# First token group of a fused convolution and MLP kernel: rows of four tokens per partition, taps transposed and added on TensorE

## Chip, cores and metric

One core of a Trainium2 chip runs the whole kernel. The metric is device time in microseconds; 1181.46 us is the median of three runs of the kernel before (1181.32 to 1181.98). A profile is one execution of the same program.

## What is computed

For each of 16384 tokens (4 sequences of 4096) a softmax over 7 taps is formed for each of 8 heads; the token's 192 features are the sum over the taps of weight times the features of the token and the six before it. The result goes through an MLP with 2048 hidden units whose activation is s * relu(h)^2 + b.

```python
w = np.exp(weight_gen - np.max(weight_gen, axis=-1, keepdims=True))
w = w / (np.sum(w, axis=-1, keepdims=True) + 1e-09)          # softmax over K = 7 taps
x_unf = x_pad[:, idx, :].reshape(B, S, K, H, group)          # the token and the six before it
x = np.einsum('bshk,bskhg->bshg', w, x_unf).reshape(B * S, D)  # D = 192, H = 8, group = 24
h = x @ w_in                                                 # w_in 192 x 2048, float64
r = np.maximum(h, 0.0)
out = ((s * (r * r) + b) @ w_out).astype(np.float32)         # w_out 2048 x 192, float64
```

## The kernel before, in words

**Tiling.** Tokens come in 32 groups of 512 (`T`), taken in the order 1 to 31, then 0. A group goes through the convolution on DVE, is transposed, and is multiplied with the weights on PE. The hidden units come in 16 blocks of 128; two blocks are a chunk (`NC` = 8 chunks), with one tile `wc[i]` per chunk that holds a high and a low part of its weights.

**Precision.** Each product is made of three fp32r matmuls: high weights by high x, low weights by high x, high weights by low x. `convert(i)` makes the parts of a chunk from the raw float64 words in four steps: Abs on ACT (L187); three DVE steps (L190 to L198); the high copy on ACT (L203) beside two DVE steps (L205, L209); six matmuls on PE (L219 to L221) that leave the low part in PSUM, and the copy of it on ACT (L222). `ahead(i, n)` issues the next n of these steps.

**Layout of a group.** In `load` a partition holds 16 tokens and 48 of the 192 features (a quarter, `q`), with six tokens of halo. `conv_pieces(g)` is a list of 15 small pieces: softmax_a, exp, softmax_b, four products (L300), five adds (L311, L319), the DVE transposes (L330, L335), split_hi on ACT (L342) and split_lo on DVE (L348). The result stands in two tiles: xa has the first 32 features of each quarter, 128 in all; xb has the other 16 of each, 64 in all, and the same 64 a second time in the other half of the partitions, put there by copies through DMA, which SP issues (L355). xb is multiplied in two halves of 64 partitions.

**Order of work.** Everything stands under `manual_schedule`: each engine, and each engine's list of DMA issues, runs in the order of the program text. SP issues nearly all transfers. First come the loads of group 0 (x by ACT's queue), the raw weights of chunks 0 and 1 (`load_weights(0)`), group 1, the raw weights of chunks 2 and 3, s and b; then group 0's convolution with chunk 0's conversion between its pieces; then a loop over the 8 chunks that does group 0's MLP (`mm1_pair`, `relu2`, `low_g`, `mm2_pair`) beside the conversion of the next chunks and the convolution of group 1. From group 1 on `mm1_quad` and `mm2_quad` take two chunks at a time. In `relu2` ACT does Relu (L443), Square (L445), then a conversion step's low copy, then gh (L449); `low_g` is one DVE instruction (L455).

**Places that the change touches.** The first loads (L535 to L541), `load_weights` (L149), `conv_pieces` (L262), `mm1_pair` (L402), the calls ahead of the chunk loop (L549 to L554), and `store` (L523). The program gives all transfers of SP and ACT eight completion semaphores, handed out in turn; a transfer is issued only when the one that had its semaphore before has landed.

Of the kernel before, what the change touches and what calls it, by code (L numbers as in the profile page):

```python
# [7 lines left out]
F32 = mybir.dt.float32  # L8
F32R = mybir.dt.float32r
# [11 lines left out]
def dynamic_conv_then_relu2_mlp(  # L21
# [24 lines left out]
    nc = tc.nc  # L46
# [27 lines left out]
    xin = ctx.enter_context(tc.tile_pool(name="xin", bufs=2))  # L74
    conv = ctx.enter_context(tc.tile_pool(name="conv", bufs=1))
# [15 lines left out]
    ORDER = list(range(1, NG)) + [0]  # L91

# [56 lines left out]
    def load_weights(k):  # L149

        r = raw.tile([P, 2, CW, 2], U32, tag="r", name="r")
        rw = r.rearrange("p c n w -> p c (n w)")
        c0 = k * QUAD * P * 2
        for q in range(Q):
            src = w_in_u[q * FQ:q * FQ + 1, c0:c0 + 1]
            nc.sync.dma_start(
                out=rw[q * 32:(q + 1) * 32, :, CA * 2:CB * 2],
                in_=bass.AP(src.tensor, src.offset, [[F * 2, 32], [2 * P * 2, 2], [1, 2 * P * 2]]),
            )
        for q in range(Q):  # L160
            for i in range(2):
                f = (q + 2 * i) % Q * FQ + 32
                c = c0 + (1 - q // 2) * P * 2
                src = w_in_u[f:f + 1, c:c + 1]
                nc.sync.dma_start(
                    out=rw[q * 32 + i * TAIL:q * 32 + (i + 1) * TAIL, :, CB * 2:CO * 2],
                    in_=bass.AP(src.tensor, src.offset, [[F * 2, TAIL], [2 * P * 2, 2], [1, P * 2]]),
                )
        for c in range(2):
            o = (k * 2 + c) * 2 * P  # L170
# [5 lines left out]
        raw_t[k] = r  # L176
# [47 lines left out]

    def constants():
# [35 lines left out]

    def conv_pieces(g):  # L262
        st = {}

        def softmax_a():
            wg = wg_t.pop(g)
            w = wg.rearrange("p j h k -> p (j h) k")
# [11 lines left out]
        def softmax_b():  # L279
# [5 lines left out]
            w = small.tile([P, J, HQ, K], F32, tag="w", name="w")  # L285
# [58 lines left out]
        def split_lo():  # L344
# [8 lines left out]
            for q in range(Q):  # L353
                o = (q + 2) % Q * 32
                nc.sync.dma_start(out=b[q * 32 + TAIL:q * 32 + 2 * TAIL], in_=b[o:o + TAIL])  # L355

            x_t[g] = [[(0, v[:, 0]), (1, v[:, 0]), (0, v[:, 1])] for v in x]

        return [
# [281 lines left out]
```

## Time and profile before

| | |
|---|---|
| median of three runs | 1181.46 us (1181.32 to 1181.98) |
| span of the profiled execution | 1178.3 us |
| PE busy | 1144.9 us, 97% |
| DVE busy | 938.2 us, 80% |
| ACT busy | 826.4 us, 70% |
| PE busy from 0 to 10, 10 to 20, 20 to 30, 30 to 40, 40 to 50 us | 0, 1.76, 4.90, 8.00, 9.14 us |

A row of the timeline gives the start in us, the length in us, the engine (PEld is PE's weight load, SPq and ACTq are DMA issues), the line, the operation, output and input by name, and a count where like instructions are merged. A bracket at its end is the idle time before it and what ended it. In a table by stage each engine has its busy time with the number of instructions behind it.

### The profile page before, as it was taken

The page shows a single profiled execution, that of the slowest core. Times are in us where ns is not written, and L with a number is a line of the kernel's source. Part 1 is how long each engine was busy: PE and PEld are TensorE (multiplying, and loading weights), DVE is VectorE, ACT ScalarE, POOL GpSimd, SP SyncE. Part 2 cuts the span into 40 slices and gives each one's busy share as a digit, 9 for nine tenths or more (in the row PEclk, how much of TensorE's full clock was granted, in tenths as well). Part 3 has the DMA queues.
Part 4 walks back from the last instruction along what each step waited for, and adds up shares of the span by engine and source line. Part 5 has one row for each costly group of instructions (what it writes and reads, how often), then busy time and mean ns, then how long its engine had stood idle before and what let it go on. Part 6 is the DMA issues. An engine that isn't in the chain of part 4 may idle for free.

```text
span 1178.3 us, 29855 instructions
## 1 busy us (share of the span) xinstructions
PE 1144.9 (97%) x12672; PEld 1034.5 (88%) x12672; DVE 938.2 (80%) x1357; ACT 826.4 (70%) x889; POOL 6.1 (1%) x22
## 2 busy tenths in 40 slices
PE   2999999999999999999999999999999999999997
PEld 1678999999999999999999999999999999999997
DVE  7988887788887778887778898777788777888843
ACT  2767767777677677776776776767767677677674
POOL 0000000000000000000000000000000000000000
PEclk9999999999999999999999999999999999999999
DMA  7421222221122222122222112222112222212110
GB/s 155 117 44 28 40 46 47 32 46 27 35 46 46 39 40 37 30 40 47 46 33 46 26 36 46 46 35 44 29 37 42 47 46 33 45 26 36 24 24 14
DMA packets 175833, 50.17 MB, mean 43 GB/s; under 512 B 165076, under 2 KB 168660, under 8 KB 175700
## 3 DMA queue, kind: packets, MB, share of 16 engines
q1 hardware_dynamic: 172820, 47.73, 22.6%
q8 instruction: 99, 1.62, 0.6%
q10 hardware_dynamic: 2880, 0.54, 0.3%
q14 instruction: 34, 0.28, 0.1%
HBM read 27.26 MB, written 12.58 MB: 34 GB/s over the span
## 4 chain that ended last, share of the span: by engine, by line
PE 95%; DVE 2%; ACT 1%; DMA 1%; SPq 0%; issue 0%
PE po L500 47%; PE ph L432 43%; PE po L482 2%; PE ph L219 1%; PE ph L408 1%; DVE pr L300 1%; PE ph L414 1%; DMA r<-in_moe_w_in_dram 0%; DVE gl L455 0%; DVE pr L311 0%; ACT gh L449 0%; PE ph L246 0%; ACT r L445 0%; SPq L101 0%; DMA xb<-xb 0%
## 5 line engine op out<-in xcount | busy, mean ns | idle before, releaser
L500 PE MATMUL po<-wc,gh 64*128 64x384 f32 x3936 | 570.5, 356 | 0.0
L500 PE MATMUL po<-wc,gl 64*128 64x192 f32 x3936 | 492.8, 247 | 0.8 <-DVE gl L455 0.8
L455 DVE TENSOR_TENSOR gl<-r,gh 128x1024 fp32r<-128x1024 f32 x256 | 313.1, 1223 | 213.1 <-ACT gh L449 206.9
L443 ACT ACTIVATE r<-ph 128x1024 f32<-128x1024 f32 x256 | 249.0, 1024 | 300.0 <-PE ph L432 295.1
L500 PEld LDWEIGHTS po<-wc,gl 64*128 64x128 f32 x3936 | 375.7, 188 | 6.3 <-DVE gl L455 1.1
L500 PEld LDWEIGHTS po<-wc,gh 64*128 64x128 f32 x3936 | 368.7, 184 | 5.1
L432 PE MATMUL ph<-xa,wc 64*128 64x512 f32 x2976 | 365.6, 391 | 0.0
L432 PEld LDWEIGHTS ph<-xa,wc 64*128 64x128 f32 x2976 | 269.8, 184 | 52.9 <-issue 0.2
L449 ACT CAST gh<-r 128x1024 fp32r<-128x1024 f32 x256 | 269.2, 1052 | 7.9
L445 ACT ACTIVATE r<-r 128x1024 f32<-128x1024 f32 x256 | 270.7, 1057 | 0.3
L300 DVE TENSOR_TENSOR pr<-xt,w 128x1152 f32<-128x1152 f32 (+1 forms) x128 | 193.6, 1554 | 2.5 <-DMA r<-in_moe_w_in_dram 0.7
L432 PE MATMUL ph<-xb,wc 64*128 64x512 f32 x1488 | 190.4, 388 | 0.0
L432 PEld LDWEIGHTS ph<-xb,wc 64*128 64x128 f32 x1488 | 139.9, 184 | 30.5
L311 DVE TENSOR_TENSOR pr<-pr 128x768 f32<-128x768 f32 (+1 forms) x128 | 145.2, 1155 | 2.1
L512 DVE SCALAR_TENSOR_TENSOR u<-po,s_sb,bias 128x192 f32<-128x192 f32 x128 | 49.8, 410 | 1.6 <-PE po L482 1.6
L518 DVE SCALAR_TENSOR_TENSOR y<-po,s_sb,u 128x192 f32<-128x192 f32 x128 | 49.8, 409 | 0.1
L219 PE MATMUL ph<-r,eye_f 128*128 128x384 f32 x32 | 15.6, 570 | 18.2 <-DVE r L198 18.2
L319 DVE TENSOR_TENSOR acc<-pr 128x768 f32<-128x768 f32 x32 | 30.6, 958 | 1.1
L330 DVE STREAM_TRANSPOSE xT<-acc 128x128 f32<-128x128 f32 x128 | 28.5, 280 | 1.1
L335 DVE STREAM_TRANSPOSE xT<-acc 128x128 f32<-128x128 f32 x128 | 27.2, 271 | 0.0
L482 PE MATMUL po<-wc,gh 128*128 128x384 f32 x80 | 23.9, 361 | 0.1
L219 PEld LDWEIGHTS ph<-r,eye_f 128*128 128x128 f32 x32 | 5.7, 205 | 20.8 <-issue 20.8
(45 smaller groups left out, 336.0 us busy)
## 6 DMA issues: line engine op xcount, KB each, us to landing
xt<-in_x_dram SPq DMA_DIRECT2D x120, 132.0 KB, 3.4
out_dram<-y SPq DMA_DIRECT2D x128, 96.0 KB, 1.9
xb<-xb SPq DMA_DIRECT2D x128, 64.0 KB
wg<-in_weight_gen_dram SPq DMA_DIRECT2D x128, 28.0 KB, 2.6
r<-in_moe_w_out_dram SPq DMA_DIRECT2D x8, 384.0 KB, 3.7
r<-in_moe_w_in_dram SPq DMA_DIRECT2D x16, 128.0 KB, 3.0
r<-in_moe_w_in_dram SPq DMA_DIRECT2D x32, 32.0 KB, 2.2
xt<-in_x_dram ACTq DMA_DIRECT2D x4, 132.0 KB, 4.0
```

What stands on the lines that cost most here:

```text
L219: nc.tensor.matmul(out=o, lhsT=eye_f, rhs=fv[:, c], start=True, stop=False)
L300: nc.vector.tensor_tensor(out=pr[:, k0:k1, :, h * G:(h + 1) * G], in0=bass.AP(xs.tensor, xs.offset, [xs.ap[0], [FQ, n], [FQ, J], [1, G]]), ...
L311: nc.vector.tensor_tensor(out=pr[:, o:o + n], in0=pr[:, o:o + n], in1=pr[:, a:a + n], op=ALU.add)
L432: nc.tensor.matmul(out=h_t[n, p][:, j], lhsT=w1(2 * k + p, part, block, j, rows), rhs=v[rows], start=(at < 2 and c == 0), stop=(at >= 4 an ...
L443: nc.scalar.activation(out=r[p], in_=h_t.pop((n, p)), func=AF.Relu)
L445: nc.scalar.activation(out=r[p], in_=r[p], func=AF.Square)
L449: nc.scalar.copy(out=gh, in_=r[p])
L455: nc.vector.tensor_tensor(out=gl, in0=sq, in1=gh.bitcast(F32), op=ALU.subtract)
L482: nc.tensor.matmul(**m)
L500: nc.tensor.matmul(**m)
L512: nc.vector.scalar_tensor_tensor(out=u[i], in0=o_t[g][tiles[i]][:, 1, :], scalar=s_sb, in1=bias, op0=ALU.mult, op1=ALU.add,)
L518: nc.vector.scalar_tensor_tensor(out=y[:, t], in0=o_t[g][t][:, 0, :], scalar=s_sb, in1=u[i - 1], op0=ALU.mult, op1=ALU.add,)
```

## The change

Group 0 of the processing order gets a path of its own. `load_rows` puts four neighbouring tokens with all 192 features (and six tokens of halo) in a partition, by one transfer for the tap weights and two for x, all on SP. The products are made for all taps by `times` (tails: features 32 to 47 of each quarter, per token; firsts: features 0 to 31, per range of taps), and `sum_taps` transposes each tap's product on PE and adds the taps in PSUM. ACT and DVE then split the sums from PSUM into xa and xb (`row_hi`, `row_lo`); the second half of xb is filled by one DMA copy on SP, asked for after the tails and ahead of the firsts. `load_weights` can take one chunk at a time and issue its block B on another queue: chunk 0's goes to ACT's queue. A one-column Exp is done right after the constants, and `awake()` puts 48 matmuls on PE. `mm1_pair` of chunk 0 does the high weights of both blocks first, then the six convert matmuls and the low copy of chunk 0, then the low weights. The store of group 0 is one transfer.

```diff
--- before.py
+++ after.py
@@ -72,6 +72,7 @@
+    rows = ctx.enter_context(tc.tile_pool(name="rows", bufs=1))
@@ -89,6 +90,23 @@
+
+    def load_rows(i):
+
+        t0 = ORDER[i] * T
+        wg = xin.tile([P, NT, H, K], F32, tag="wg", name="wg")
+        nc.sync.dma_start(
+            out=wg.rearrange("p a h k -> p (a h k)"),
+            in_=wgf[t0:t0 + T, :].rearrange("(p a) n -> p (a n)", a=NT),
+        )
+        xt = rows.tile([P, NT + HALO, D], F32, tag="xr", name="xr")
+        src = xf[t0 - HALO:t0 - HALO + 1, :]
+        for a0, a1 in ((0, 2 * NT - 1), (2 * NT - 1, NT + HALO)):
+            nc.sync.dma_start(
+                out=xt[:, a0:a1].rearrange("p a d -> p (a d)"),
+                in_=bass.AP(src.tensor, src.offset + a0 * D, [[NT * D, P], [1, (a1 - a0) * D]]),
+            )
+        xt_t[i], wg_t[i] = xt, wg
@@ -146,34 +164,47 @@
-    def load_weights(k):
...
+    def load_weights(k, chunks=(0, 1), side=nc.sync):
+
+        if k not in raw_t:
+            raw_t[k] = raw.tile([P, 2, CW, 2], U32, tag="r", name="r")
+        a, n = chunks[0], len(chunks)
+        rw = raw_t[k].rearrange("p c n w -> p c (n w)")
+        c0 = (k * 2 + a) * 2 * P * 2
+        rw = rw[:, a:a + n]
+
+        def block_a(q):
+            f = q * FQ
+            src = w_in_u[f:f + 1, c0:c0 + 1]
             nc.sync.dma_start(
...
+                in_=bass.AP(src.tensor, src.offset, [[F * 2, 32], [2 * P * 2, n], [1, 2 * P * 2]]),
+            )
+        def block_b(q, i):
+            f = (q % 2 + 2 * i) * FQ + 32
+            c = c0 + (1 - q // 2) * P * 2
+            src = w_in_u[f:f + 1, c:c + 1]
+            side.dma_start(
+                out=rw[q * 32 + i * TAIL:q * 32 + (i + 1) * TAIL, :, CB * 2:CO * 2],
+                in_=bass.AP(src.tensor, src.offset, [[F * 2, TAIL], [2 * P * 2, n], [1, P * 2]]),
+            )
...
+        for q in range(Q):
+            block_a(q)
+        for q in range(Q):
+            for i in range(2):
+                block_b(q, i)
+        for c in range(n):
+            second_weights(c)
@@ -222,6 +253,14 @@
+    spare = const.tile([P, 1], F32, name="spare")
+
+    def awake():
+
+        ph = ps_h.tile([P, 2, T], F32, tag="h1", name="ph")
+        for _ in range(48):
+            nc.tensor.matmul(out=ph[:, 0, 0:P], lhsT=eye, rhs=ones, start=True, stop=True)
@@ -259,11 +298,78 @@
+    def parts_of(x):
+        return [[(0, v[:, 0]), (1, v[:, 0]), (0, v[:, 1])] for v in x]
...
+        def times(out, f, k0, n, slot, m, each, width):
+
+            xs, ws = xt_t[g][:, k0 + slot:k0 + slot + 1, f:f + 1], st["w"][:, slot:slot + 1, f // G:f // G + 1, k0:k0 + 1]
+            nc.vector.tensor_tensor(
+                out=out,
+                in0=bass.AP(xs.tensor, xs.offset, [xs.ap[0], [D, n], [each * G, m], [1, width]]),
+                in1=bass.AP(ws.tensor, ws.offset, [ws.ap[0], [1, n], [each * K, m], [0, width]]),
+                op=ALU.mult,
+            )
+
+        def sum_taps(i, k0, k1, a):
+            m = (P, P // 2)[i]
+            for k in range(k0, k1):
+                nc.tensor.matmul(
+                    out=st["ps"][i][0:m, a * P:(a + 1) * P], lhsT=st["p"][i][:, k, a], rhs=eye_f,
+                    is_transpose=True, start=(k == 0 and a == 0), stop=(k == K - 1), skip_group_check=True,
+                )
+
+        def row_tails(a):
+            def f():
+                if a == 0:
+                    pr = conv.tile([P, K * NT * D], F32, tag="pr", name="pr")
+                    n = K * NT * P
+                    st["p"] = [v.rearrange("p (k a n) -> p k a n", k=K, a=NT) for v in (pr[:, 0:n], pr[:, n:])]
+                    st["ps"] = [ps_o.tile([P, T], F32, tag=f"o{i}", name="px") for i in range(2)]
+                out = st["p"][1][:, :, a].rearrange("p k (o e n) -> p k o e n", o=2, e=2)
+                for e in range(2):
+                    times(out[:, :, :, e], 32 + e * 2 * FQ, 0, K, a, 2, 2, TAIL)
+                sum_taps(1, 0, K, a)
+            return f
+
+        def row_firsts(k0, k1):
+            def f():
+                out = st["p"][0][:, k0:k1].rearrange("p k a (q n) -> p k (a q) n", q=Q)
+                times(out[:, :, :, 0:G], 0, k0, k1 - k0, 0, NT * Q, 2, G)
+                times(out[:, :, :, G:32], G, k0, k1 - k0, 0, NT * Q, 2, 32 - G)
+                for a in range(NT):
+                    sum_taps(0, k0, k1, a)
+            return f
+
+        R = [slice(0, P), slice(0, P // 2)]
+
+        def row_hi(i):
+            def f():
+                if "x" not in st:
+                    st["x"] = [xtp.tile([P, 2, T], F32R, tag=n, name=n) for n in ("xa", "xb")]
+                nc.scalar.copy(out=st["x"][i][R[i], 0], in_=st["ps"][i][R[i]])
+            return f
+
+        def row_lo(i):
+            def f():
+                x = st["x"][i]
+                nc.vector.tensor_tensor(
+                    out=x[R[i], 1], in0=st["ps"][i][R[i]], in1=x[R[i], 0].bitcast(F32), op=ALU.subtract
+                )
+                if i == 1:
+                    b = x.bitcast(F32)
+                    nc.sync.dma_start(out=b[P // 2:P], in_=b[0:P // 2])
+                else:
+                    xt_t.pop(g)
+                    x_t[g] = parts_of(st["x"])
+            return f
@@ -351,11 +457,18 @@
-                o = (q + 2) % Q * 32
-                nc.sync.dma_start(out=b[q * 32 + TAIL:q * 32 + 2 * TAIL], in_=b[o:o + TAIL])
-
-            x_t[g] = [[(0, v[:, 0]), (1, v[:, 0]), (0, v[:, 1])] for v in x]
-
+                i = (1 - q // 2) * TAIL
+                o = (q + 2) % Q * 32 + i
+                nc.sync.dma_start(out=b[q * 32 + i:q * 32 + i + TAIL], in_=b[o:o + TAIL])
+
+            x_t[g] = parts_of(x)
+
+        if g == 0:
+            return [
+                softmax_a, exp, softmax_b, row_tails(0), row_tails(1), row_tails(2), row_tails(3), row_hi(1),
+                row_lo(1), row_firsts(0, 2), row_firsts(2, 4), row_firsts(4, 6), row_firsts(6, 7),
+                row_hi(0), row_lo(0),
+            ]
@@ -396,25 +509,26 @@
-    def mm1_pair(n, p):
+    def mm1_pair(n, p, between=None):
 
         g, k = divmod(n, NQ)
         new_h(n, p, "h0")
-        for j in range(2):
-            for c, (part, v) in enumerate(x_t[g][0]):
-                nc.tensor.matmul(
-                    out=h_t[n, p][:, j], lhsT=w1(2 * k + p, part, 0, j, slice(0, P)), rhs=v,
-                    start=(c == 0), stop=False,
-                )
-        for c, (part, v) in enumerate(x_t[g][1]):
-            for j, rows in enumerate(HALVES[::-1]):
-                nc.tensor.matmul(
-                    out=h_t[n, p][:, j], lhsT=w1(2 * k + p, part, 1, j, rows), rhs=v[rows],
-                    start=False, stop=(c == 2),
-                )
+        turns = [(0, (0, 1, 2)), (1, (0, 1, 2))] if between is None else [
+            (0, (0, 2)), (1, (0, 2)), (0, (1,)), (1, (1,))
+        ]
+        left = 6
+        for at, (block, cs) in enumerate(turns):
+            if at == 2:
+                between()
+            for c in cs:
+                part, v = x_t[g][block][c]
+                left -= 1
+                for j, rows in enumerate(HALVES[::-1]):
+                    rows = rows if block else slice(0, P)
+                    nc.tensor.matmul(
+                        out=h_t[n, p][:, j], lhsT=w1(2 * k + p, part, block, j, rows), rhs=v[rows],
+                        start=(at == 0 and c == 0), stop=(left == 0),
+                    )
     def outputs(g):
-        o_t[g] = [ps_o.tile([P, 2, D], F32, tag=f"o{t}", name="po") for t in range(NT)]
+        banks = [ps_o.tile([P, T], F32, tag=f"o{t}", name="po") for t in range(NT)]
+        o_t[g] = [o[:, 0:2 * D].rearrange("p (a d) -> p a d", a=2) for o in banks]
@@ -523,7 +638,12 @@
-        g = ORDER[g]
+        i, g = g, ORDER[g]
+        if i == 0:
+            nc.sync.dma_start(
+                out=out[g * T:(g + 1) * T, :].rearrange("(p a) d -> p a d", a=NT)[:, t0:t1], in_=y[:, t0:t1]
+            )
+            return
 
     with tc.manual_schedule():
-        load(0, nc.scalar)
         constants()
-        load_weights(0)
+        load_rows(0)
+        nc.scalar.activation(out=spare, in_=ones_f[:, 0:1], func=AF.Exp)
+        load_weights(0, (0,), nc.scalar)
+        load_weights(0, (1,))
         load(1)
         load_weights(1)
         nc.sync.dma_start(out=s_sb, in_=s.partition_broadcast(P))
@@ -546,17 +668,19 @@
             for _ in range(n if i < NC else 0):
                 next(parts[i])
 
-        run_pieces(0, 0, 2)
+        awake()
+        run_pieces(0, 0, 7)
         ahead(0, 1)
-        run_pieces(0, 2, 7)
-        ahead(0, 3)
+        run_pieces(0, 7, 8)
+        ahead(0, 1)
+        run_pieces(0, 8, 15)
+        ahead(0, 1)
         ahead(1, 1)
-        run_pieces(0, 7, 15)
 
         beside = ((2, 4), (4, 5), (5, 7), (7, 8), (8, 10), (10, 12), (12, 14), (14, 15))
         for i in range(NC):
             n, p = divmod(i, 2)
-            mm1_pair(n, p)
+            mm1_pair(n, p, (lambda: ahead(0, 1)) if i == 0 else None)
```

## Rows read from the trace of the kernel before

**Rows 1.** Page, busy us of each engine, share of the span, instructions.

```profile
PE 1144.9 (97%) x12672; PEld 1034.5 (88%) x12672; DVE 938.2 (80%) x1357; ACT 826.4 (70%) x889; POOL 6.1 (1%) x22
```

**Rows 2.** Table by stage: stretch, length, busy of PE, PEld, DVE, ACT, POOL; clock; DMA; GB/s.

```profile
20.00:30.00 10.00, 4.90 (x12) 3.09 (x11) 9.75 (x18) 2.85 (x4) 0.00 (x0) 1.00 0.54 133
200.00:400.00 200.00, 200.00 (x2298) 182.71 (x2296) 161.93 (x235) 144.44 (x156) 1.33 (x4) 1.00 0.22 38
```

**Rows 3.** Waits of PE from 0 to 110 us: who for whom, us, times, longest.

```profile
...
PE ph L408 <- ACT xa L342: 5.1, 1, 5.1
PE ph L414 <- DMA xb<-xb: 1.3, 1, 1.3
PE po L482 <- DVE gl L455: 0.9, 1, 0.9
PE po L500 <- DVE gl L455: 0.8, 1, 0.8
...
```

**Rows 4.** Timeline of PE, 17 to 45 us.

```profile
18.24 1.62 PE L219 MATMUL ph<-r,eye_f 128*128 128x384 f32 x2 [18.24 <-DVE r L198]
...
21.90 0.53 PE L221 MATMUL ph<-v,eye 128*128 128x384 f32 x1
27.52 2.93 PE L408 MATMUL ph<-xa,wc 128*128 128x512 f32 x6 [5.10 <-ACT xa L342]
31.79 1.06 PE L414 MATMUL ph<-xb,wc 64*128 64x512 f32 x6 [1.34 <-DMA xb<-xb]
32.78 0.94 PE L219 MATMUL ph<-r,eye_f 128*128 128x384 f32 x2
...
34.76 0.34 PE L221 MATMUL ph<-v,eye 128*128 128x384 f32 x1
...
43.80 1.58 PE L408 MATMUL ph<-xa,wc 128*128 128x512 f32 x6
```

**Rows 5.** Timeline of DVE, 5 to 25 us.

```profile
6.01 0.39 DVE L269 TENSOR_REDUCE mx<-wg 128x32 f32<-128x224 f32 x1 [4.19 <-DMA wg<-in_weight_gen_dram]
...
10.12 5.96 DVE L300 TENSOR_TENSOR pr<-xt,w 128x1536 f32<-128x1536 f32 x4 [0.73 <-DMA r<-in_moe_w_in_dram]
16.00 0.55 DVE L190 TENSOR_SCALAR t<-t 128x768 f32<-128x768 f32 x1
...
17.18 0.96 DVE L198 SCALAR_TENSOR_TENSOR r<-r,t 128x768 uint32<-128x768 uint32 x1
...
19.64 4.48 DVE L311 TENSOR_TENSOR pr<-pr 128x1536 f32<-128x1536 f32 x4
```

**Rows 6.** Timeline of ACT and its DMA issues, the start and 37 to 41 us.

```profile
0.81 5.42 ACTq L121 DMA_DIRECT2D xt<-in_x_dram  x4
5.91 0.32 ACTq L121 DMA_DIRECT2D xt<-in_x_dram  x1
6.26 1.28 ACT L277 ACT_TABLE_LOAD   x1 [6.26 <-DMA wg<-in_weight_gen_dram]
...
37.07 0.88 ACT L203 CAST wc<-r 128x768 fp32r<-128x768 f32 x1
...
40.65 0.78 ACT L222 CAST wc<-ph 128x768 fp32r<-128x768 f32 x1
```

**Rows 7.** Waits of SP's DMA issues from 0 to 30 us.

```profile
SPq L165 <- DMA r<-in_moe_w_in_dram: 1.4, 4, 0.6
```

**Rows 8.** Timeline of SP's DMA issues, 0 to 30 us.

```profile
0.81 2.74 SPq L101 DMA_DIRECT2D wg<-in_weight_gen_dram  x4
...
18.43 3.78 SPq L165 DMA_DIRECT2D r<-in_moe_w_in_dram  x8
...
23.75 0.43 SPq L541 DMA_DIRECT2D b_sb<-in_moe_b_dram  x1
27.45 2.48 SPq L355 DMA_DIRECT2D xb<-xb  x4
```

**Rows 9.** Table by stage, columns as in Rows 2: the stretch with the highest GB/s.

```profile
24.00:26.00 2.00, 0.00 (x0) 0.00 (x0) 1.93 (x7) 0.07 (x1) 0.00 (x0) 1.00 0.95 347
```

More of the change, by code (lines that the diff above doesn't have):

```diff
@@ L147, in dynamic_conv_then_relu2_mlp, with second_weights @@
     w_out_u = w_out.bitcast(U32)
-    def load_weights(k):
[L151 to L155, printed above, removed]
+    def load_weights(k, chunks=(0, 1), side=nc.sync):
[8 more added lines that the diff above has]
+            src = w_in_u[f:f + 1, c0:c0 + 1]
             nc.sync.dma_start(
                 out=rw[q * 32:(q + 1) * 32, :, CA * 2:CB * 2],
-                in_=bass.AP(src.tensor, src.offset, [[F * 2, 32], [2 * P * 2, 2], [1, 2 * P * 2]]),
+                in_=bass.AP(src.tensor, src.offset, [[F * 2, 32], [2 * P * 2, n], [1, 2 * P * 2]]),
             )
[L160 to L167, printed above, removed]
-                )
-        for c in range(2):
-            o = (k * 2 + c) * 2 * P
+        def block_b(q, i):
[6 more added lines that the diff above has]
+            )
+        def second_weights(c):
+            o = (k * 2 + a + c) * 2 * P
             src = w_out_u[o:o + 1, 0:1]
@@ L175, in load_weights @@
             )
-        raw_t[k] = r
+        for q in range(Q):
[5 more added lines that the diff above has]
+            second_weights(c)
     def convert(i):
@@ L265, in softmax_a @@
         def softmax_a():
             wg = wg_t.pop(g)
+            st["shape"] = wg.shape
             w = wg.rearrange("p j h k -> p (j h) k")
@@ L284, in softmax_b @@
             nc.vector.reciprocal(out=sm, in_=sm)
-            w = small.tile([P, J, HQ, K], F32, tag="w", name="w")
+            w = small.tile(list(st["shape"]), F32, tag="w", name="w")
             nc.vector.tensor_tensor(
@@ L397, in new_h @@
         h_t[n, p] = ps_h.tile([P, 2, T], F32, tag=tag, name="ph")
-    def new_o(g, t):
-        o_t[g][t] = ps_o.tile([P, 2, D], F32, tag=f"o{t}", name="po")
-    def mm1_pair(n, p):
+    def mm1_pair(n, p, between=None):
         g, k = divmod(n, NQ)
         new_h(n, p, "h0")
-        for j in range(2):
-            for c, (part, v) in enumerate(x_t[g][0]):
-                nc.tensor.matmul(
-                    out=h_t[n, p][:, j], lhsT=w1(2 * k + p, part, 0, j, slice(0, P)), rhs=v,
-                    start=(c == 0), stop=False,
-                )
-        for c, (part, v) in enumerate(x_t[g][1]):
-            for j, rows in enumerate(HALVES[::-1]):
-                nc.tensor.matmul(
-                    out=h_t[n, p][:, j], lhsT=w1(2 * k + p, part, 1, j, rows), rhs=v[rows],
-                    start=False, stop=(c == 2),
-                )
+        turns = [(0, (0, 1, 2)), (1, (0, 1, 2))] if between is None else [
[14 more added lines that the diff above has]
+                    )
     def mm1_quad(n):
```

## The prediction

> **What bounds the kernel now.** I read the page first: TensorE (PE) is busy for 97% of the span [rows 1], so only what PE waits for, or extra work of PE, can move the time. The table by stage shows where the waits are: in a middle stretch PE is busy 200.00 of 200.00 us, in 20 to 30 us only 4.90 of 10 [rows 2]. Everything the change touches lies ahead of 45 us, so its worth is how much earlier or later PE gets into its unbroken run. PE's waits up to 110 us say what holds it: 5.1 us for ACT's xa (the end of group 0's convolution), 1.3 us for the DMA xb<-xb, 0.9 and 0.8 us for gl [rows 3]. The reader should then read the PE timeline: the first six xa matmuls at 27.52, the first xb ones at 31.79, after the copy has landed, chunk 1's convert matmuls from 32.78 to 34.76 + 0.34 = 35.1, and no idle after 41.6 except the 0.8 [rows 4]. From there on the order of work is the same in both kernels. As anchor I take the moment at which ACT can begin the low copy of chunk 1 (L222): 35.1 now. From it hang gh, exp, softmax_b, two products and gl of chunk 0, in this order, and PE's last early wait is for that gl [rows 3]. A shift of the anchor is a shift of the end.
>
> One more thing stands in the PE rows: the same six matmuls take 2.93 us at 27.52 and 1.58 at 43.80, and the convert matmuls 4.19 us at 18.24 (to 21.90 + 0.53 = 22.43) against 2.32 at 32.78 [rows 4]. The granted clock reads 1.00 throughout [rows 2], yet the factor of 1.8 is that of the two levels, 1.2 and 2.4 GHz; I go by the durations and call them slow and fast. Before 27.52 PE had been idle for 5.1 us; before 31.79, which is fast, for 1.3 [rows 3].
>
> **What goes.** Four products of 5.96 us stay as products (the same 5376 elements per partition in 16 smaller instructions). Five adds (4.48 us for the first four, [rows 5]) and the eight DVE transposes go, from a DVE that is the chain ahead of 27.52. Their work passes to 56 PE transposes (7 taps x 4 tokens x 2 blocks) that add up in PSUM. The table load of 1.28 us [rows 6] moves ahead of the exp, beside the loads: free. Edits with one answer: later groups' xb copies keep their number and size and only read other rows, group 0's store is one transfer and not four, po takes a whole bank: none of it adds work to PE, nothing each; if the store's SP time were in the way it would shrink.
>
> **When the x parts are ready.** (1) wg is now one transfer; the last of four, the end of the 2.74 us from 0.81 [rows 8], left at 2.9 and had landed for 6.01 [rows 5]: 3.1 from issue. Now 0.81 + 3.1 = 3.9, and with two instructions of 0.39 for softmax_a 4.7. (2) exp stands on ACT behind a new row of eight issues (chunk 0's block B), from 2.4 on (after the table load and the spare exp). The program hands round eight completion semaphores over SP's and ACT's transfers, so a ninth issue waits till the first has landed: ACT's fourth xt left at 5.91 only, as the last wg landed [rows 6], and SP stood 1.4 us in its block-B issues [rows 7]. Eight issues at 0.47 (SP's 3.78/8, [rows 8]) to 1.36 (5.42/4, [rows 6]) end between 6.2 and 13; with two large x transfers in flight I take 9. exp and softmax_b took from 7.54 (6.26 + 1.28) to 9.39 (10.12 less 0.73 of waiting) [rows 5, 6], 1.85: now 10.9. (3) Tails: 8 products of 224 elements, 0.36 each (0.39 for such a row [rows 5], a little overlapped): 13.8. (4) Three conversion steps of chunk 0, 16.00 to 18.14 [rows 5]: 15.9; row_lo(1), 0.7 by the 0.78 of 768 columns from PSUM [rows 6]: 16.6. (5) Firsts: 3584 elements at 1.11 ns (5.96 us for 5376 [rows 5]) and eight starts: 4.3, to 20.9. (6) The PE transposes of the firsts from 17.5, 28 x 0.2 (below): 23.1; row_hi(0) and row_lo(0), 0.7 each: x ready at R = 24.5. Now PE starts on xa at 27.52.
>
> A transpose that adds is nowhere in this trace. Bounds of one of 128 columns: at the rate of the xa matmuls (2.93/6 for 512 columns) 0.12 us slow and 0.07 fast; at the fp32 rate of L219 (4.19 less four matmuls of 384 columns at 0.37, halved, a third) 0.45 slow, and 0.25 fast by the same sum on 2.32 [rows 4]. I take 0.2, near the lower end with something for a weight load each. The 48 matmuls of awake() run from 1.9 for some 5 us at 0.11, while PE has nothing else: free.
>
> **The copy xb<-xb, which decides.** Now it is four issues on SP from 27.45, which SP had been waiting for: its list was empty at 23.75 + 0.43 = 24.2 [rows 8]. In the new order row_lo(1) asks for it at 16.6, but load(1), load_weights(1), s and b stand ahead of it on SP, which takes its list in order. Count: now 42 issues until 24.2; then 45 (wg 1, x 2 and not 4; block A of chunk 0 and 1 apart, 4 more). Without stalls: 24.2 - 1.4 (stalls of now) - 1.1 (2.74 for four wg, 1.65 for three) + 4 x 0.47 (3.78/8, [rows 8]) = 23.6. The stalls grow: wg and x are 1.1 MB; at the 347 GB/s of the best two microseconds [rows 9] from 2.2 on they are through at 5.4 and seen at about 6.1, and SP's next issues wait for them (about +1.8), while ACT's eight take every second semaphore (about +1.5). So the copy is issued at 26.9. It lands 2.5 us after its issue now (the last of four began at 29.3, PE went on at 31.79); as one of 256 KB behind two of 384 KB I add 0.4. L = 29.8; bounds 26.1 (no stall) and 32.
>
> **The new order on PE.** mm1_pair of chunk 0 now runs xa with the high weights (turn 1), then xb (turn 2, needs L), then chunk 0's convert matmuls, then the low weights. The convert matmuls, long done by 22.43 before, stand behind the wait for the copy. After L: four xb matmuls, 1.06 x 4/6 = 0.7 fast, x 1.85 = 1.3 slow; convert 2.32 fast, 4.19 slow; low copy on ACT 0.85. X, the end of that copy, is L + 3.9 fast and L + 6.3 slow. After R turn 1 takes 2.0 slow (four of six in 2.93) and ends at 26.5, so PE is idle 3.3 us before L, between the idle stretch that came out slow (5.1) and the one that came out fast (1.3) and nearer to the first; I take slow xb and a convert half way (3.25): X = 29.8 + 1.3 + 3.25 + 0.85 = 35.2. Then ACT does hi(1), Abs(2), relu, square in order before the low copy of chunk 1; these are the steps from 37.07 to 40.65 now, 3.5 us [rows 6]. PE needs no longer (1.1 and 2.32). Anchor: 35.2 + 3.5 = 38.7, against 35.1: **3.6 us later**. What DVE saved is lost there: it has run through softmax_a of group 1 and stands waiting for Abs(2). The later loads come no later against X than now, and SP has landed chunk 2 by then.
>
> The span is 1178.3, the median 1181.46; the 3.2 between are launch and end, which the change leaves alone. 1181.46 + 3.6 = 1185.1.
>
> A rule that bears on the clock stands in the Trainium skill, TensorE: Matmul & The Clock Gate, section Part 4: PE-mode transpose: it says that the fast clock does not engage for transposes. Then the 56 of them would leave PE slow, all of convert would be 4.19 and the time 0.9 later, 1186.0, inside the forecast's own range. No row of before has a transpose on PE.
>
> **Rivals.** (B) The same chain, but the stalls stay away or the clock is fast: L = 26.1 to 29.8, so that X is 30.0 to 33.8 and the time 1.6 us earlier to 2.2 later, 1179.9 to 1183.7, which is no change. For it: SP stood only 1.4 us before. (C) The other side, faster: the copy is out so early that R decides. PE would then do turns 1 and 2 (1.1 + 0.7), convert (2.3) and the low copy (0.85) after R, fast; with exp not held by ACT's issues R is 22, X = 26.9, 4.7 us earlier: 1176.8. It decides once the copy lands before turn 1 ends, 23 here; against it stands SP's count of 45 issues, which at 0.47 are never under 21 us. (D) The transposes run at the fp32 rate: at 0.45 the tails end at 24, the firsts near 39, X is 47.5 and the time 1197; at 0.25 R is about 29 and the time 1185 to 1187, beside the forecast. For it: the fp32 matmuls of this trace do run so. The same page's section Terms names a transpose mode four times faster for fp32, which speaks against D; by it a transpose would take 0.11 slow.
>
> **How the numbers follow.** Forecast 0.50 (1183.9 to 1188.5), B 0.27, C 0.12, D 0.11. A change of 0.2% (2.4 us) is about what a measurement of this kernel can tell from none. Faster: C but for a hundredth, 0.11; same: B and that hundredth, 0.28; slower: forecast and D, 0.61. The range takes in forecast and B, and leaves out most of C and the upper part of D: 1180.0 to 1188.5; the forecast's own is 1183.9 to 1188.5.
>
> **What would show it.** In the new trace: the xb copy of group 0 issued by SP at 25 to 28 with its list full up to it (right), or near 17 (C). PE idle 3 us or more before the first xb matmul, released by the DMA. The convert matmuls of chunk 0 after that and of 4 us (slow) or 2.3. Transposes of 0.1 to 0.2 us. exp at 9. The low copy of chunk 1 on ACT near 38.7. PE unbroken after that, as now. Wrong would be an x part later than the copy, or a wait of PE behind 50 us that is not there now.

## The result, and the profile after

| | before | after |
|---|---|---|
| median of the runs | 1181.72 us (1181.32 to 1182.13, 4 runs) | 1196.47 us (1195.58 to 1199.5, 4 runs) |
| ratio | | 1.0129, 95% interval 1.0114 to 1.0143 |
| span of the profiled execution | 1178.3 us | 1193.9 us |
| ACT's low copy of chunk 1 (the anchor) | 35.1 us | 42.7 us |
| one step of two chunks in the loop, from xa to xa | 8.72 us | 8.79 us |

The change makes the kernel 14.75 us slower; 3.6 were forecast. The direction and the mechanism at the start came out as written; its size was twice what was forecast, and a second loss of the same size lies behind 50 us, where the prediction has no term.

The kernel before took 1179.7 to 1180.2 us in some executions and 1181.3 to 1182.6 in most, its profile (span 1178.3; a run's time is 1.7 to 1.8 above its span) is one of the first sort, and one execution of g4 that took 1569 us at a granted clock of 0.656 is left out of the comparisons.

The page, busy us of each engine (answers to [rows 1]):

```profile
PE 1172.4 (98%) x12776; PEld 1052.6 (88%) x12776; DVE 931.9 (78%) x1356; ACT 825.6 (69%) x890; POOL 6.1 (1%) x22
```

PE is busy 27.5 us longer, and the 104 instructions more (48 of `awake()`, 56 transposes) are 10.50 + 5.50 + 4.91 = 20.9 of it. The table by stage, columns as in [rows 2]:

```profile
20.00:30.00 10.00, 6.11 (x32) 5.36 (x32) 6.39 (x13) 2.25 (x3) 0.00 (x0) 0.83 0.85 162
30.00:40.00 10.00, 5.14 (x16) 2.90 (x16) 3.15 (x5) 1.58 (x3) 0.00 (x0) 0.66 0.20 70
200.00:400.00 200.00, 200.00 (x2284) 181.41 (x2282) 164.63 (x240) 142.32 (x152) 1.33 (x4) 1.00 0.23 38
```

The reader is to see three things: PE is busy for half of 30 to 40 us; the granted clock, the first number behind POOL's, is 0.83 and 0.66 there (0.50 is 1.2 GHz, 1.00 is 2.4); and in the long stretch, where it is busy 200.00 of 200.00 us as before, it does fewer instructions (2284 for 2298). PE's waits up to 110 us (who for whom, us, times, longest; answers to [rows 3]) and its timeline (answers to [rows 4]):

```profile
PE ph L528 <- DMA xb<-xb: 6.3, 1, 6.3
PE px L320 <- DVE pr L310: 2.6, 1, 2.6
...
PE po L597 <- DVE gl L569: 1.1, 1, 1.1
PE po L615 <- DVE gl L569: 0.7, 1, 0.7
```

```profile
1.74 10.50 PE L262 MATMUL ph<-ones,eye 128*128 128x128 f32 x48 [1.74 <-DVE eye L271]
12.04 5.50 PE L320 MATMUL px<-eye_f,pr 128*64 128x128 f32 x28
20.12 4.91 PE L320 MATMUL px<-eye_f,pr 128*128 128x128 f32 x28 [2.59 <-DVE pr L310]
26.49 1.20 PE L528 MATMUL ph<-xa,wc 128*128 128x512 f32 x4 [1.46 <-ACT wc L234]
33.98 1.22 PE L528 MATMUL ph<-xb,wc 64*128 64x512 f32 x4 [6.29 <-DMA xb<-xb]
35.13 1.65 PE L250 MATMUL ph<-r,eye_f 128*128 128x384 f32 x2
...
38.05 0.34 PE L252 MATMUL ph<-v,eye 128*128 128x384 f32 x1
...
51.38 1.59 PE L528 MATMUL ph<-xa,wc 128*128 128x512 f32 x6
```

The 5.1 us for xa are gone, and 6.3 us for the copy stand in their place. The SP timeline (answers to [rows 8]) and its waits say why, and ACT's (answers to [rows 6]) what follows:

```profile
2.22 6.46 SPq L179 DMA_DIRECT2D r<-in_moe_w_in_dram  x4
...
28.72 0.43 SPq L663 DMA_DIRECT2D b_sb<-in_moe_b_dram  x1
29.27 0.54 SPq L364 DMA_DIRECT2D xb<-xb  x1
```

```profile
SPq L179 <- DMA xr<-in_x_dram: 4.4, 1, 4.4
```

```profile
8.42 0.39 ACT L383 ACTIVATE e<-e 128x224 f32<-128x224 f32 x1 [6.12 <-DMA r<-in_moe_w_in_dram]
...
38.42 0.80 ACT L253 CAST wc<-ph 128x768 fp32r<-128x768 f32 x1 [9.66 <-PE ph L252]
...
42.71 0.80 ACT L253 CAST wc<-ph 128x768 fp32r<-128x768 f32 x1
```

```profile
18.18 0.68 DVE L359 TENSOR_TENSOR xb<-px,xb 64x512 fp32r<-64x512 f32 x1 [2.82 <-ACT xb L353]
```

DVE ended xb's low part at 18.18 + 0.68 = 18.9. SP, whose list was never empty from 2.22 on, came to the copy at 29.27, and PE went on at 33.98. ACT's first low copy (chunk 0) begins at 38.42, the second (chunk 1) at 42.71. Chunk 2's first xa matmuls begin at 51.38, before at 43.80 [rows 4]: 7.58 us of the loss are there by then. The span is 15.6 longer, so 8.0 come later, in a stretch where PE waits no more than before (1.5 us in all, before 1.6). PE's groups from 200 to 1100 us (form, count, busy us, mean ns, idle), first before, then after:

```profile
L500 PE MATMUL po<-wc,gh 64*128 64x384 f32 x3296 | 477.7, 356 | 0.0
L432 PE MATMUL ph<-xa,wc 64*128 64x512 f32 x2486 | 305.3, 391 | 0.0
L432 PE MATMUL ph<-xb,wc 64*128 64x512 f32 x1242 | 159.0, 388 | 0.0
```

```profile
L615 PE MATMUL po<-wc,gh 64*128 64x384 f32 x3276 | 475.0, 356 | 0.0
L546 PE MATMUL ph<-xa,wc 64*128 64x512 f32 x2458 | 306.3, 394 | 0.0
L546 PE MATMUL ph<-xb,wc 64*128 64x512 f32 x1236 | 160.3, 391 | 0.0
```

The second layer's matmuls (po) take the same 356 ns; the first layer's, whose moving operands are xa and xb, take 394 and 391 for 391 and 388, though line, shape and clock (1.00) are the same. Matmuls overlap, so the cost is read from starts: the time from the first of the 36 matmuls of a step (24 xa, 12 xb) to the matmul behind the last of them, as a mean over the 68 or 69 complete steps between 300 and 900 us, is 4157 ns before and 4222 ns after. This number is called the first-layer time below. 31 groups of four steps make 124 x 0.065 = 8.1 us.

What can change the speed of an instruction that is itself unchanged? The change adds two tiles, `xr` with (4 + 6) x 192 x 4 = 7680 bytes of a partition and the one-column `spare`, and all tiles allocated behind them move by 7712 bytes, a slot of 32 bytes for the one column included. So theory: two losses that add, 8.0 us by the late copy and some 8 by the place of the x tiles in a partition. Rivals: the late copy makes the loop slower too, in a way that PE's waits don't show; or something else that the change does to the loop (group 0's store, the rows that the later copies read) does.

### The profile page after: what moved, and what is told of

It reads as the page before. It is cut to its first block, busy times and chain, and to the rows that moved or that the text cites. A ratio compares the mean times of both kernels' runs of the same rounds, so it can differ in the third digit from the quotient of the medians.

```text
span 1193.9 us, 30070 instructions
## 1 busy us (share of the span) xinstructions
PE 1172.4 (98%) x12776; PEld 1052.6 (88%) x12776; DVE 931.9 (78%) x1356; ACT 825.6 (69%) x890; POOL 6.1 (1%) x22
## 4 chain that ended last, share of the span: by engine, by line
PE 96%; DVE 1%; ACT 1%; DMA 0%; issue 0%; POOL 0%; ACTq 0%; POOLq 0%
PE po L615 47%; PE ph L546 43%; PE po L597 2%; PE ph L528 1%; PE ph L262 1%; PE px L320 1%; PE ph L250 1%; DVE gl L569 0%; DMA xb<-xb 0%; ACT gh L563 0%; ACT r L559 0%; ACT r L557 0%; PE ph L285 0%; PE ph L252 0%; PE ph L251 0%
## 5 line engine op out<-in xcount | busy, mean ns | idle before, releaser
L546 PE MATMUL ph<-xa,wc 64*128 64x512 f32 x2976 | 371.0, 394 | 0.0
L546 PE MATMUL ph<-xb,wc 64*128 64x512 f32 x1488 | 193.0, 391 | 0.0
L406 DVE TENSOR_TENSOR pr<-xt,w 128x1536 f32<-128x1536 f32 (+1 forms) x124 | 187.5, 1553 | 1.8 <-DVE w L392 0.6
L417 DVE TENSOR_TENSOR pr<-pr 128x1536 f32<-128x1536 f32 (+1 forms) x124 | 140.7, 1154 | 2.1
L597 PE MATMUL po<-wc,gl 128*128 128x192 f32 x80 | 20.4, 254 | 1.9 <-DVE gl L569 1.9
L454 DVE TENSOR_TENSOR xa<-xT,xa 128x512 fp32r<-128x512 f32 x31 | 21.2, 684 | 0.0
```

Source lines behind the costliest of these rows:

```text
L406: nc.vector.tensor_tensor(out=pr[:, k0:k1, :, h * G:(h + 1) * G], in0=bass.AP(xs.tensor, xs.offset, [xs.ap[0], [FQ, n], [FQ, J], [1, G]]), ...
L417: nc.vector.tensor_tensor(out=pr[:, o:o + n], in0=pr[:, o:o + n], in1=pr[:, a:a + n], op=ALU.add)
L546: nc.tensor.matmul(out=h_t[n, p][:, j], lhsT=w1(2 * k + p, part, block, j, rows), rhs=v[rows], start=(at < 2 and c == 0), stop=(at >= 4 an ...
L597: nc.tensor.matmul(**m)
```

## The experiments

No run leaves a part of the work out. Times in this table are medians; "step" is the first-layer time in ns.

| run | x tiles moved by | copy on | median us | ratio to before, 95% interval | step |
|---|---|---|---|---|---|
| after | 7712 = 30 x 256 + 32 | SP | 1196.47 | 1.0114 to 1.0143 | 4222 |
| e1_pad64 | 7744 = 30 x 256 + 64 | SP | 1194.78 | 1.0098 to 1.0132 | 4206 |
| e3_copy_act | 7712 | ACT | 1188.47 | 1.0045 to 1.0075 | 4222 |
| e4_pad64_copy_act | 7744 | ACT | 1186.77 | 1.0031 to 1.0061 | 4206 |
| h1_pad512 | 8192 = 32 x 256 | SP | 1187.52 | 1.0032 to 1.0065 | 4157 |
| g1_pad512_copy_act | 8192 | ACT | 1179.80 | 0.9979 to 0.9998 | 4157 |
| g4_no_awake | 8192 | ACT | 1178.92 | 0.9969 to 0.9988 | 4157 |
| h2_early_exp | 8192 | ACT | 1177.72 | 0.9953 to 0.9979 | 4157 |
| e2_before_32 | 32, with all behind | SP | 1190.30 | 1.0061 to 1.0091 | 4222 |
| g2_x_only_32 | 32 | SP | 1187.32 | 1.0033 to 1.0073 | 4218 |
| g3_behind_x_32 | 0 (those behind: 32) | SP | 1181.69 | 0.9991 to 1.0012 | 4158 |
| h3_x_only_256 | 256 | SP | 1181.00 | 0.9986 to 1.0005 | 4157 |
| h4_x_only_128 | 128 | SP | 1188.16 | 1.0033 to 1.0067 | 4218 |

The last five are the kernel before with unused tiles put in; the others are the changed kernel.

**e1_pad64**: is a place on a multiple of 64 bytes enough? (The Exp goes to the first of the 16 columns.)

```diff
-    spare = const.tile([P, 1], F32, name="spare")
+    spare = const.tile([P, 16], F32, name="spare")
```

> The changed kernel with the new one-column tile of the constants widened to 16 columns, so that every tile after it moves by 64 bytes in place of 32; nothing else. In the changed kernel a step of two chunks in the middle of the run takes 8.785 us against 8.720 before, and the difference lies in the matmuls that read xa and xb, whose addresses became 32 off a multiple of 64. Theory (the 32 bytes do it): the step is back at 8.72, PE's 24 xa matmuls at 2.95 us, and the time falls by about 124 x 0.065 = 8.1 us, from 1196.5 to 1188.4. Rival (the move by 7.7 KB, or the whole bank for po, does it): step 8.785 and 1196.5 as they are. The late start of the first group (low copy of chunk 1 at 42.7 us) stays under both.

1194.78 us, where 1188.4 was expected. It is not enough: the step went from 4222 to 4206 ns only. That a multiple of 64 bytes will do is refuted; that the place counts is not.

**e2_before_32**: the other way round, the kernel before with nothing but a one-column tile ahead of the others.

```diff
+    spare = const.tile([P, 1], F32, name="spare")
     def constants():
         nc.gpsimd.memset(ones_f, 1.0)
+        nc.gpsimd.memset(spare, 0.0)
```

> The kernel before with one more one-column tile among the constants (and a memset of it), which moves all later tiles by 32 bytes and changes nothing else. Theory (the 32 bytes): the step goes from 8.720 to 8.785 us, the time from 1181.5 to about 1189.6. Rival (7.7 KB or po's bank): both unchanged, 1181.5.

1190.30 us and the 4222 ns of after, with no transposes, no new load and the copies where they were. So the second loss doesn't need the change's work; 32 bytes make it. In e2's trace the granted clock is also 0.50 from 24.9 to 35.1 us, and the first xb matmuls take 1.74 us for 1.06 [rows 4]:

```profile
31.74 1.74 PE L417 MATMUL ph<-xb,wc 64*128 64x512 f32 x6 [1.30 <-DMA xb<-xb]
```

That is not the move's doing. In the trace of g3 below, where the x tiles stay, the clock is as low from 25.3 to 35.5 us and the same matmuls take 1.74 us; its span is 1180.0 us, e2's 1188.0. The 8.0 between these two are the place.

**e3_copy_act**: the first loss alone. ACT issues the copy and SP's list doesn't matter to it.

```diff
-                    nc.sync.dma_start(out=b[P // 2:P], in_=b[0:P // 2])
+                    nc.scalar.dma_start(out=b[P // 2:P], in_=b[0:P // 2])
```

> The changed kernel with the copy xb<-xb of the first group issued by ACT and not by SP; nothing else. Theory (the copy stands at the end of SP's list): it is issued near 19, PE's wait of 6.3 us for it goes, the first xb matmul comes near 27.6, the low copy of chunk 0 ends near 33 in place of 39.2, and the time falls by about 6 us, from 1196.5 to 1190.3. Rival (another wait stands right behind, the convert matmuls or ACT's order): the copy is early but the time falls by under 2 us, to 1194.5 or more.

1188.47 us, 8.0 less than after. ACT's timeline and PE's:

```profile
18.77 0.52 ACTq L364 DMA_DIRECT2D xb<-xb  x1
...
35.19 0.78 ACT L253 CAST wc<-ph 128x768 fp32r<-128x768 f32 x1
```

```profile
26.30 1.19 PE L528 MATMUL ph<-xa,wc 128*128 128x512 f32 x4 [1.46 <-ACT wc L234]
27.42 0.73 PE L528 MATMUL ph<-xb,wc 64*128 64x512 f32 x4
28.08 0.94 PE L250 MATMUL ph<-r,eye_f 128*128 128x384 f32 x2
```

The copy leaves at 18.77 and nobody waits for it. xb follows xa at once, everything from there on runs at the high clock's rate, and the anchor is 35.19: 7.5 less than after, and what it was before. That the gain is 8.0 and not the expected 6.2 is the clock: PE has no 6.3 us of idle in which it falls, and the xb and convert matmuls, 1.22 and 3.26 us in after, take 0.73 and 2.3 (28.08 to 30.38).

**e4_pad64_copy_act**: both edits together.

> Both edits together, the 64-byte tile and the copy on ACT. Theory (two causes that add): 1196.5 - 8.1 - 6.2 = 1182.2, which is the kernel before within a microsecond: then these two make up the whole loss. Rival (a third cause, or one hides the other): 1185 or more.

1186.77 us, 8.0 less than e1: the copy is worth the same at another place of the tiles. The 1182.2 expected was missed, by the part that 64 bytes didn't give back.

**g1_pad512_copy_act** and **h1_pad512**: `spare` of 128 columns makes the move 8192 bytes; g1 with the copy on ACT, h1 with it on SP.

> The changed kernel with the copy xb<-xb on ACT and the new tile of the constants widened to 512 bytes, so that all later tiles move by 8192 bytes against the kernel before (7680 of them the new x tile). So far a shift by 32 of the kernel before gave the same intervals between the matmuls of xa and xb as the changed kernel's shift of 7712 = 15 x 512 + 32 (228, 234, 228 ns), and the shift by 7744 = 15 x 512 + 64 others. Theory (the place of the x tiles within 512 bytes sets the pace): a step of two chunks is 8.72 us again and the time 1188.5 - 8.1 = 1180.4. Rival (the move by 7.7 KB costs too, or the pace depends on other things): step 8.77 to 8.79 and 1186 to 1188.

> The changed kernel with the one-column tile widened to 512 bytes, so that all later tiles lie a multiple of 512 bytes (8192) behind where they lay before; the copy xb<-xb stays on SP. Theory (two separate causes, late copy and place of the x tiles, which add): the place is back, so a step of two chunks takes 8.72 us, and only the late copy stays: 1196.5 - 8.1 = 1188.4, 1187.4 to 1189.4. Rival (the late copy's 8 us are in part the place's, they do not add): below 1186 or above 1191.

1179.80 and 1187.52 us, both with 4157 ns. With after and e3 they are a square:

| | moved by 7712 | moved by 8192 | place |
|---|---|---|---|
| copy on SP | 1196.47 | 1187.52 | 8.95 |
| copy on ACT | 1188.47 | 1179.80 | 8.67 |
| late copy | 8.00 | 7.72 | |

The two losses add within 0.3 us. h1 has the late copy, the new store and the later copies' other rows, and its step is 4157 ns: the rivals named above, which would slow the loop by these, are out. The place costs 0.6 to 0.9 more than 124 steps of 65 ns; group 0, which runs the same matmuls in smaller parts, has its share of that, and the rest is not resolved. In h1's profiled execution PE's wait for the copy was 6.5 us and the clock stayed at half from 29.6 to 46.6 us; that execution took 1190.85 us, the three others 1186.7 to 1187.6.

**g2_x_only_32** and **g3_behind_x_32**: which tiles? The kernel before with 32 bytes ahead of the x tiles and 480 behind them (only xa and xb move), and with 32 bytes behind them (only the tiles behind them move, which hold the activations). The diff is g2's, without the tiles that fill the two pools; g3 has `pad1` alone.

```diff
+    pad0 = ctx.enter_context(tc.tile_pool(name="pad0", bufs=1))
     xtp = ctx.enter_context(tc.tile_pool(name="xtp", bufs=2))
+    pad1 = ctx.enter_context(tc.tile_pool(name="pad1", bufs=1))
     act = ctx.enter_context(tc.tile_pool(name="act", bufs=3))
```

> The kernel before with 32 bytes put ahead of the tiles xa and xb and 480 behind them: those two alone are moved by 32, all tiles behind by 512. Theory (the x tiles' place): the step is 8.785 us as with everything moved by 32, the time near 1189.6. Rival (the place of the act and g tiles, which DVE and ACT write meanwhile): step 8.72, 1181.5.

> The counterpart: 32 bytes put behind xa and xb, so that the act, g and y tiles move by 32 and the x tiles stay. Theory (the x tiles' place): step 8.72 us, time 1181.5. Rival: 8.785 and 1189.6.

1187.32 (two runs) and 1181.69 us. Moving the tiles behind costs nothing, moving the x tiles makes the loss: it is the place of the x tiles. But g2's step, 4218 ns, and time are less than the 1189.6 expected from e2: its span is 1186.4 us for e2's 1188.0, at the same low clock up to 35 us. From xa to xa a step of two chunks takes 8.773 us in g2, 8.787 in e2 and 8.720 in before and g3. So with the x tiles off their place, the place of those behind them matters a little too (some 1.6 us); why was not tried.

**h3_x_only_256** and **h4_x_only_128**: the same with 256 bytes ahead of the x tiles and 256 behind them, and with 128 and 384.

> The kernel before with 256 bytes of unused tile ahead of the x tiles and 256 behind them, so that only xa and xb move, by 256 bytes. Theory 1 (only the place within 256 bytes or less counts): 36 matmuls of the first layer in 4157 ns, 1181.5. Theory 2 (the place within 512 bytes counts, and the place of before is one of the good ones): 4206 to 4222 ns and 1186 to 1188. Either way the prologue is that of before.

> The kernel before with 128 bytes of unused tile ahead of the x tiles and 384 behind them, so that only xa and xb move, by 128 bytes. A move by 256 left the kernel as it was, one by 32 and one by 64 more than that (with everything else) did not. Theory 1 (the place counts within 128 bytes): 36 matmuls of the first layer in 4157 ns, 1181 to 1182. Theory 2 (it counts within 256 bytes): some 4206 to 4222 ns and 1186 to 1188.

1181.00 and 1188.16 us. PE's groups from 200 to 1100 us, first h3, then h4:

```profile
L439 PE MATMUL ph<-xa,wc 64*128 64x512 f32 x2486 | 305.3, 391 | 0.0
L439 PE MATMUL ph<-xb,wc 64*128 64x512 f32 x1242 | 159.0, 388 | 0.0
```

```profile
L439 PE MATMUL ph<-xa,wc 64*128 64x512 f32 x2472 | 307.2, 394 | 0.0
L439 PE MATMUL ph<-xb,wc 64*128 64x512 f32 x1236 | 160.6, 392 | 0.0
```

A move by 256 changes nothing, one by 128 as much as one by 32. With the 8192 of g1, every move by a multiple of 256 bytes that was tried left the step at 4157 ns, and each of the others (32, 64, 128 over such a multiple) made it 4206 to 4222. The kernel before stood at a good place.

**g4_no_awake**: g1 without the call of `awake()`.

> As the kernel with the 512-byte tile and the copy on ACT, without the 48 matmuls of awake(). They took 10.5 us on PE (1.74 to 12.24), longer than the products needed, so the first transposes waited for them. Theory A (they only stand in the way): transposes begin at 10.6 in place of 12.0, x is ready 1.4 us earlier, the time falls by about 1.4. Theory B (they are what makes the clock fast by 15.3 us): without them the xa, xb and convert matmuls of chunk 0 run slow, some 3 to 5 us more, and the time rises by 2 to 3 us in sum.

1178.92 us, 0.9 less than g1; the two intervals overlap. Theory B is out, and the 1.4 of theory A isn't shown. PE's timeline:

```profile
11.03 6.14 PE L320 MATMUL px<-eye_f,pr 128*64 128x128 f32 x28 [11.03 <-DVE pr L310]
19.76 5.00 PE L320 MATMUL px<-eye_f,pr 128*128 128x128 f32 x28 [2.59 <-DVE pr L310]
26.21 1.20 PE L528 MATMUL ph<-xa,wc 128*128 128x512 f32 x4 [1.46 <-ACT wc L234]
```

Without the 48 matmuls the transposes start 1.0 us earlier than in after, and the first 28 take longer (0.219 us for 0.196 each), because the granted clock rises to 2.4 GHz at 17.0 us in g4 and at 16.7 in after, just before they end. The xa matmuls still run at the high rate, 1.20 us for four. With `awake()` at work from 1.74 us on, the clock rose at 16.7 (after), 15.9 (h1) and 14.2 (g1), so its 48 matmuls did not bring it up by their end at 12.24. No gain of `awake()` is shown here.

**h2_early_exp**: a version that gets more out of the early copy. g4, with softmax_a and exp between the first four and the last four of ACT's block-B issues, the firsts of four taps ahead of chunk 0's conversion, and the raw weights of chunks 2 and 3 ahead of group 1. (The diff is against after, without the edits of g1 and without the hook in `load_weights`.)

```diff
-        load_weights(0, (0,), nc.scalar)
+        load_weights(0, (0,), nc.scalar, lambda: run_pieces(0, 0, 2))
...
+        load_weights(1)
         load(1)
-        load_weights(1)
...
-        awake()
-        run_pieces(0, 0, 7)
-        ahead(0, 1)
-        run_pieces(0, 7, 8)
-        ahead(0, 1)
-        run_pieces(0, 8, 15)
+        run_pieces(0, 2, 7)
+        run_pieces(0, 9, 11)
+        ahead(0, 2)
+        run_pieces(0, 7, 9)
+        run_pieces(0, 11, 15)
```

> As the run with 512 bytes and the copy on ACT, without awake(); softmax_a and exp of group 0 stand between the first four and the last four of ACT's block-B issues; the firsts of four taps stand ahead of chunk 0's Abs and DVE conversion steps; the raw weights of chunks 2 and 3 are loaded ahead of group 1. Theory (with the copy early, the order of work up to the first xa matmul decides the time): exp at 4 and not 8, first xa matmul near 19 to 21 and not 24.3, low copy of chunk 1 on ACT at 29 to 31 and not 34: 1174.5 to 1177.5, best guess 1176. Rival (the later raw weights or ACT's own work decide, the early part is hidden): within 0.8 of 1179.

1177.72 us, 1.2 less than g4 (the intervals overlap) and 0.34% less than before; 1.7 above the best guess and 0.2 above the range expected. Its timeline, ACT, PE and DVE:

```profile
3.82 0.39 ACT L385 ACTIVATE e<-e 128x224 f32<-128x224 f32 x1 [1.52 <-DVE e L379]
...
7.12 6.73 PE L322 MATMUL px<-eye_f,pr 128*64 128x128 f32 x44 [7.12 <-DVE pr L312]
16.62 1.96 PE L322 MATMUL px<-eye_f,pr 128*128 128x128 f32 x12 [2.77 <-DVE pr L312]
20.03 2.07 PE L530 MATMUL ph<-xa,wc 128*128 128x512 f32 x4 [1.45 <-ACT wc L236]
...
29.17 0.39 DVE L377 TENSOR_REDUCE mx<-wg 128x32 f32<-128x224 f32 x1 [3.10 <-DMA wg<-in_weight_gen_dram]
...
30.40 0.80 ACT L255 CAST wc<-ph 128x768 fp32r<-128x768 f32 x1
...
36.74 1.22 DVE L571 TENSOR_TENSOR gl<-r,gh 128x1024 fp32r<-128x1024 f32 x1
...
38.01 0.52 PE L599 MATMUL po<-wc,gl 128*128 128x192 f32 x1 [2.24 <-DVE gl L571]
...
41.79 1.58 PE L530 MATMUL ph<-xa,wc 128*128 128x512 f32 x6
```

exp at 3.82, xa at 20.03 and the anchor at 30.40 are as expected, 4.7 us ahead of g4's 35.10. But group 1's wg, now loaded later, lets DVE wait 3.1 us; softmax_b of group 1 and a product stand ahead of gl on DVE, and PE waits 2.2 us for gl, 1.1 in g4. Behind that wait the granted clock is 0.50 from 38.1 to 41.5 us, and the second-layer matmuls up to chunk 2 take 3.8 us (38.01 to 41.79), 2.2 in g4 (41.55 to 43.74). So chunk 2's xa matmuls begin only 1.95 ahead of g4's. The anchor stopped being the last thing that PE waits for: 1.1 us of the gain went to a longer wait and 1.6 to the clock that was low behind it. And the four xa matmuls took 2.07 us, the low clock's rate.

## Why the prediction was wrong, point by point

**Right: what decides at the start.** The wait for xa is replaced by one for the copy, the copy stands behind SP's full list, and the convert matmuls stand behind the copy. From the copy's landing to the end of chunk 0's low copy it took 39.22 - 33.98 = 5.2 us (5.4 in the sum), with the xb matmuls at 1.22 (1.3) and the convert matmuls from 35.13 to 38.39, 3.26 (3.25), half slow and half fast, as chosen. That half is luck: the granted clock rose at 37.2 in this execution, and in h1's, where it rose at 46.6, the same matmuls ran from 34.77 to 38.97, 4.2, all slow. From there to the anchor 3.5 (3.5). Transposes took 0.196 and 0.175 us as a mean (0.2): rival D is out. From start to start they took 0.213 us at the low clock and 0.109 at the high one; the prediction's 0.11 for the low one is that of the high one. exp stood at 8.42 (9).

**Wrong in size: the copy's issue and landing.** The step "so the copy is issued at 26.9 ... L = 29.8" failed: 29.27 and 33.98. SP's stalls are 29.27 - 23.6 = 5.7 us by the prediction's own count, for 3.3; 4.4 of them are one wait, for the second x transfer, issued at 1.74 and landed 6.1 us later, near 7.8; the sum had x seen at about 6.1, and so 1.8 for the wait. The landing took 4.7 us after the issue for 2.9; in the other traces with this one copy of 256 KB it took 4.3 (g1) to 5.8 (e3). Even the outer bound, 32, was too low. Anchor: +7.6 for +3.6. e3 and g1 show that this term alone is 7.7 to 8.0 us of the time.

**Wrong: "From there on the order of work is the same in both kernels ... A shift of the anchor is a shift of the end".** The order is the same, the duration of the work is not. The prediction listed what each edit adds for PE to do, and "none of it adds work to PE, nothing each" was taken as the whole. The two new tiles were never costed as what they also are, a move of xa and xb by 30 x 256 + 32 bytes. That is 8.7 to 8.95 us by the square, more than the late copy, and put at nothing without a reason; no row of before could have priced it, but the range had no room for it either. Its sign of error was named ("a wait of PE behind 50 us"), its form was not: there is no wait, PE is just slower while fully busy.

**Wrong without effect on the time of after: x ready at R = 24.5.** It was 26.38. The sum let DVE set the end of the tails (13.8, then the conversion) and counted only the firsts' transposes on the path. But PE could start on the tails at 12.04 only, after `awake()`, priced at 5 us and free and in fact 10.50, and the 28 tail transposes then took 5.50, to 17.5; DVE waited 2.82 us for the xb that ACT copies from them. With the copy at 33.98 this decides nothing; with the copy on ACT it is on the path.

**Wrong without effect on the 3.6: "the 3.2 between are launch and end".** A run's time is 1.7 to 1.8 above its span; the other 1.5 lie between the median and the profiled execution of before. g3's trace, with the order and the step of before and a span of 1180.0, shows where: the granted clock is 0.50 from 25.3 to 35.5 us, and chunk 2's xa begin at 45.45 for 43.80 [rows 4]. In the trace of before the records of the clock begin with its rise at 31.2 us, so the 1.00 that [rows 2] gives ahead of it is no reading; that the prediction went by durations there was right.

**A rule against the rows.** The Trainium skill, TensorE: Matmul & The Clock Gate, section Part 4: PE-mode transpose, says that the fast clock does not engage for transposes. The traces of g4 and h2 contradict it: transposes are PE's only work there up to xa, and the granted clock rises to 2.4 GHz while they run. In h2 it rises at 10.8 us, among the first 44, and their starts, 0.213 us apart until then, come 0.109 apart; after 2.8 us without work it falls to 1.2 GHz at 17.6, among the other 12, and is back at 24.4, behind the four xa matmuls (2.07 us). In g4 it rises at 17.0, as the first 28 end, falls at 20.4 after 2.6 us without work, and rises at 23.9 among the other 28; the four xa matmuls at 26.21 then took 1.20 us (at 1.2 GHz six took 2.93 [rows 4]). So transposes do raise the clock; what the xa matmuls meet is a matter of when the clock last fell.

**The sum.** Against 1181.72: the place +8.95, the late copy +7.7 (h1 less g1), the rest of the change -1.9 (g1 against the same 1181.72; against the runs beside it -1.4). Together 14.75, the measured loss; they run from after to before in three steps, so this sum could not come out otherwise, and what carries the first two is that the square's other sides give 8.67 and 8.00. The rest is no loss; that the new path itself gains is not shown. The -1.9 is about what the low clock of the start costs in g3's trace (1.65), and against the trace of before, which is without it, g1's span of 1177.4 us is 0.9 less and g4's 1178.3 the same. Two losses that are not part of the change's idea hide a path that, as far as these runs show, is worth little either way.

## What to carry to other kernels

Where PE is busy all the time, look at the durations of unchanged instructions in a long stretch before looking for waits; a new tile ahead of others can move operands and cost as much as a lost transfer. Keep the place of a tuned kernel's moving operands by a multiple of 256 bytes (a wider unused tile is enough) before a change is judged. A transfer that the next step needs goes on a queue with a short list, and an early gain counts only up to the next thing loaded late.

## What the runs showed of the hardware

- The first-layer time depends on where xa and xb begin in a partition: 4157 ns after moves by 0, 256 and 8192 bytes, 4218 to 4222 after 32 and 128 over a multiple of 256, 4206 after 64 over one. Which of the two tiles counts, how it depends on the shape (64 rows, 512 columns, fp32r, two matmuls side by side), why, and why the tiles behind add to it (e2 against g2), was not tried. The second layer's matmuls kept their 356 ns (355 to 356) in after, g1, g2, h3 and h4.
- Transposes that add in PSUM in float32, 128 columns, weight load included, start 0.213 us apart while the granted clock is 0.50 and 0.109 apart while it is 1.00 (after, g4, h1, h2), and the clock rose while PE did nothing else (g4, h2).
- 48 matmuls of 128 columns with a weight load each took 10.50 us, also 0.213 from start to start, with nothing else on PE: twice the price worked out from the long matmuls.
- After 6.3 us without work PE's four xb matmuls ran in 1.22 us, at the low rate (granted clock 0.50 from 30.4 us), for 0.73 without the wait (e3); how long the low rate then lasted differs between the two traces with that wait (to 37 us in that of after, to 46.6 in that of h1).
